# Linear attention with a sine-gated MLP on one core: the first quarter of w_in by a hardware queue in fp32, the first k by the software queue, and x stored batch by batch

## The chip, the cores and the metric

The kernel runs on 1 core of one Trainium2 chip, in one launch. The metric is the device time in microseconds (us) of one execution. The core has five engines that work side by side: PE (matrix products), DVE, ACT and POOL (elementwise work), and SP, which here only starts transfers. Loads and stores are moved by 16 DMA engines. SP and ACT start transfers on hardware queues; POOL starts them on the software queue, and a transfer on it may change the type from fp32 to bf16 on its way.

## The reference

```python
# q, k, v: [4 batches, 8 heads, 768 positions, 64]; lam: [8]
for b in range(12):                      # blocks of 64 positions
    intra = (qb @ kb.T * Dmask) @ vb     # Dmask[i, j] = lam ** (i - j) for i >= j, else 0
    inter = (qb * lam ** (i + 1)) @ kv_state
    out[block] = intra + inter
    kv_state = lam ** 64 * kv_state + (kb * lam ** (63 - i)).T @ vb
x = out as [3072 tokens, 512]
h = x @ w_in                             # w_in: [512, 2048]
s = sin(alpha * h)
g = h + s * s / (alpha + 1e-9)
y = g @ w_out                            # w_out: [2048, 512]; y is the result, fp32
```

All inputs and the result are fp32 in memory. The kernel computes its products in bf16.

## The kernel before, in words

The 768 positions are cut into 6 chunks of 128 (NT = 6). One chunk of all 4 batches is a group of 512 tokens. For each group the attention gives x (`xt`), then 16 units `hidden(g, f)` (f from 0 to 15) compute h for 128 columns of w_in each, and `project(g, m, part)` multiplies the result `gall` with w_out. The order of all work is written out by hand: the text of the kernel is the order of each engine's instructions. The attention of chunk t + 1 and the projections of group g - 1 are placed between the hidden units of group g.

**Start-up (lines 66 to 129).** SP's hardware queue loads k of chunk 0, batch 0 as fp32 into `raw_k`, ACT's hardware queue loads q of batch 0 into `raw_q` (L79 to L81). POOL then starts six loads of 128 KB (bf16 in SBUF), k and q of batches 1 to 3 (L112 to L114), two loads of v with 256 KB each (batches 0 and 1, then 2 and 3, L115), w_in's first quarter in two halves (L117, L118), and its other three quarters (L119). The software queue works through them in this order.

**Chunk 0 (lines 499 to 543).** DVE casts `raw_k` to bf16 (L502) and scales `raw_q` (L503). For each batch, PE transposes k and q (`turn`, L261), ACT copies the results to SBUF (L267), PE computes the scores and DVE multiplies them by the decay table C0 into an `STm` tile (`scores1`, L286; pool `work`, 3 buffers, L49). `outs` (L297) multiplies `STm` by v and writes x of that batch into `xt`: batch 0 by ACT (L304), batches 1 to 3 by DVE (L306). There are 4 batches and 3 `STm` buffers. `spin` (L493) issues matrix products on a constant tile whose results are not used; such calls stand at the beginning (nine of 512 columns) and between the steps. `decay_tables` (L170) computes, on ACT, tables of powers of lam; L128, four of its instructions, is read nowhere. L538 loads ACT's table for the sine.

**Hidden units (L429).** One unit is 4 products of 512 columns (L433, one for each 128 rows of w_in), the sine on ACT (L436), a square on ACT (L441) or on DVE (L449; `squarer`, L422, chooses), and the sum on DVE into `gall` (L450). `xt` is laid out as [128, 4 parts of the feature dimension, 512 tokens], so that a product reads 512 adjacent elements per partition. In group 0, units 1, 3, 5, 7, 9 and 13 have their square on DVE.

**POOL after the start-up (lines 544 to 554).** w_out's first quarter, a product `kdec` (L226) of chunk 0, loads of chunk 1, another `kdec`, the table C64 (L187), further quarters of w_out and loads of chunk 1, in this order; casts of the state (L330) follow. POOL waits where it stands for a tile that has not landed, and starts no transfer that is written behind.

Of the kernel before, what the change touches and what calls it, by code (L numbers as in the profile page):

```python
# [15 lines left out]
def kernel(  # L16
# [26 lines left out]
    consts = ctx.enter_context(tc.tile_pool(name="consts", bufs=1))  # L43
    wpool = ctx.enter_context(tc.tile_pool(name="wts", bufs=1))
    rawp = ctx.enter_context(tc.tile_pool(name="raw", bufs=1))
    qkp = ctx.enter_context(tc.tile_pool(name="qk", bufs=2))
    vp = ctx.enter_context(tc.tile_pool(name="vv", bufs=3))
    trp = ctx.enter_context(tc.tile_pool(name="trans", bufs=2))
    work = ctx.enter_context(tc.tile_pool(name="work", bufs=3))  # L49
    kdp = ctx.enter_context(tc.tile_pool(name="kdec", bufs=2))  # L50
    kvp = ctx.enter_context(tc.tile_pool(name="kvstate", bufs=2))
    xtp = ctx.enter_context(tc.tile_pool(name="xt", bufs=2))
# [14 lines left out]
    HALF = (LO, HI)  # L67
# [3 lines left out]
    qn, kn, vn = {}, {}, {}  # L71
    NAT = {"k": (kn, k), "q": (qn, q), "v": (vn, v)}
# [2 lines left out]
        for d, nm, p in ((qn, "qn", qkp), (kn, "kn", qkp), (vn, "vn", vp)):  # L75
            d[t] = p.tile([P, B, H, D], BF16, name=nm)

    raw = {}
    for nm, eng in (("k0", nc.sync), ("q0", nc.scalar)):  # L79
        raw[nm] = rawp.tile([P, H, D], FP32, name=f"raw_{nm}")  # L80
        eng.dma_start(out=raw[nm][:], in_=NAT[nm[0]][1][0, :, 0:T, :].rearrange("h p e -> p h e"))  # L81
    alpha_fp = consts.tile([NFC, P], FP32, name="alpha_fp")

    w_in_sb = [wpool.tile([P, NDC, 512], BF16, name=f"w_in{i}") for i in range(4)]
    w_out_sb = [wpool.tile([P, 4, DM], BF16, name=f"w_out{i}") for i in range(4)]

    def load_w_in(i, w0=0, w1=512):
        w = slice(512 * i + w0, 512 * i + w1)
        nc.gpsimd.dma_start(out=w_in_sb[i][:, :, w0:w1], in_=moe_w_in[:, w].rearrange("(c p) g -> p c g", p=P))

    def load_w_out(i):
        nc.gpsimd.dma_start(out=w_out_sb[i][:],
# [2 lines left out]
    def load(t, nm, b0, b1):  # L95
        dst, src = NAT[nm]
        to = dst[t][:, b0:b1, :, :].rearrange("p b h e -> p (b h) e")
        by_head = src[b0:b1, :, t * T:(t + 1) * T, :].rearrange("b h p e -> p (b h) e")
        n = H * (b1 - b0)
        if t and nm != "v" and b0 == 2:  # L100
            nc.gpsimd.dma_start(out=to[:, 0:n - 1, :], in_=by_head[:, 1:n, :])
            nc.gpsimd.dma_start(out=to[:, n - 1:n, :], in_=by_head[:, 0:1, :])
        else:
            nc.gpsimd.dma_start(out=to, in_=by_head)  # L104
# [4 lines left out]
    dist = consts.tile([P, T], FP32, name="dist")  # L109
    nc.gpsimd.iota(out=dist[:], pattern=[[1, T]], base=0, channel_multiplier=-1,  # L110
                   allow_small_or_imprecise_dtypes=True)
    for b in range(1, B):  # L112
        for nm in "kq":
            load(0, nm, b, b + 1)  # L114
    for b in (0, 2):  # L115
        load(0, "v", b, b + 2)
    load_w_in(0, 0, 256)  # L117
    load_w_in(0, 256, 512)  # L118
    for i in range(1, 4):  # L119
        load_w_in(i)  # L120

# [26 lines left out]
    lnlam = consts.tile([P, H + 2], FP32, name="lnlam")  # L148
# [15 lines left out]
    Etab = consts.tile([P, HP, T], FP32, name="Etab")  # L164
    Eb = Etab[:, :, 0:D].unsqueeze(1).broadcast_to([P, 2, HP, D])
    L64 = consts.tile([P, 2, HP], FP32, name="L64")
    L128 = consts.tile([P, 2, HP], FP32, name="L128")
    later = {}

    def decay_tables():  # L170
        nc.scalar.copy(out=lnlam[:, H:H + 2], in_=lnlam[:, 0:2])
        later["R128"] = powers("R128", 2, lnlam[:], [P, H + 2])
        later["NE64"] = powers("NE64", 3, lnlam[:].rearrange("p (hp hd) -> p hd hp", hd=2), [P, 2, HE])
        later["R64"] = powers("R64", 4, lnlam[:], [P, H + 2])
        for L, n in ((L128, T), (L64, D)):
            for pr in range(2):
                for hd, half in enumerate(HALF):
                    nc.scalar.activation(out=L[half, pr, :], in_=lnlam[half, pr + hd:pr + hd + H - 1:2],
                                         func=ACTF.Exp, scale=float(n))

    def etab(*cs):
        for c in cs:
# [11 lines left out]
    V, G, A = nc.vector, nc.gpsimd, nc.scalar  # L194
    xt = {}
# [17 lines left out]
        return SB[2 if blk else t % 2]  # L213

    def new_xt(t):
        xt[t] = xtp.tile([P, NDC, GRP], BF16, name="xt")

    def xview(t):
        return xt[t][:].rearrange("p c (b k i) -> p b k c i", b=B, k=2)

    def decay_k(t, b0, b1):
        if t not in kdec:
# [48 lines left out]
    def halves(hd):  # L271
        return slice(hd * D, (hd + 1) * D)
# [24 lines left out]
    def outs(t, b, n, eng=None):  # L297
        O = bank("O_ps", n)[:].rearrange("p (c i) -> p c i", c=HP)
        for h in range(H):
            nc.tensor.matmul(out=O[halves(h % 2), h // 2, :], lhsT=vn[t][:, b, h, :], rhs=STm[t, b][:, h % 2, h // 2, :],  # L300
                             start=(h < 2), stop=True, skip_group_check=True)
        x = xt[t][:, :, b * T:(b + 1) * T]
        if eng is nc.scalar:
            nc.scalar.copy(out=x, in_=O)  # L304
        else:
            nc.vector.tensor_tensor(out=x, in0=O, in1=Etab[:], op=ALU.mult)  # L306
# [114 lines left out]

    def squarer(g, f):  # L422
        if g == 0:
            return V if f in (1, 3, 5, 7, 9, 13) else A
        return A

    H0 = (0, 1, 2, 3, 5, 6, 7, 0, 1, 2, 5, 0, 1, 2, 0, 1)
# [1 line left out]
    def hidden(g, f, between=None):  # L429
        hps = bank("hps", H0[f] if g == 0 else (5, 6, 4)[f] if g == 1 and f < 3 else AB[0] if g == 1 and f == 15 else AB[f + 1] if g == 2 and f < 2 else (1, 0, 2)[(f + 2) % 3] if g == 1 and f > 6 else HB[(16 * g + f + 1) % 3])  # L430
        w = w_in_sb[f // 4]
        for c in range(NDC):
            nc.tensor.matmul(out=hps[:], lhsT=w[:, c, (f % 4) * P:(f % 4 + 1) * P],  # L433
                             rhs=xt[g][:, c, :], start=(c == 0), stop=(c == NDC - 1))
# [58 lines left out]
    def spin(n, bk, cols=256):  # L493
        ps = bank("hps", bk)
        for _ in range(n):
            nc.tensor.matmul(out=ps[:, 0:cols], lhsT=fill[:, 0:P], rhs=fill[:, 0:cols], start=True, stop=True)  # L496
# [1 line left out]

    new_xt(0)
    new_turned(0)  # L500
    spin(9, 0, 512)
    nc.vector.tensor_copy(out=kn[0][:, 0, :, :], in_=raw["k0"][:])  # L502
    nc.vector.tensor_tensor(out=qn[0][:, 0, :, :], in0=raw["q0"][:], op=ALU.mult,  # L503
                            in1=Rq[:].unsqueeze(2).broadcast_to([P, H, D]))
    nc.vector.tensor_tensor(out=C0[:], in0=tri[:].unsqueeze(1).unsqueeze(1).broadcast_to([P, 2, HP, T]),
                            in1=NE[:].unsqueeze(3).broadcast_to([P, 2, HP, T]), op=ALU.mult)
# [29 lines left out]
    outs(0, 1, 1)  # L536
    warm = consts.tile([P, 1], FP32, name="warm")
    nc.scalar.activation(out=warm[:], in_=lnlam[:, 0:1], func=ACTF.Sin)  # L538
    spin(2, 6)
    outs(0, 2, 2)  # L540
    spin(2, 6)
    outs(0, 3, 0)
    spin(5, 6)
    load_w_out(0)
    decay_k(0, 0, 2)
    for nm in "kq":
# [185 lines left out]
```

## Time and profile before

| | |
|---|---|
| median of 3 runs | 210.94 us (210.92 to 210.99) |
| the profiled execution's own time | 210.92 us |
| its span in the profile | 209.1 us |
| PE busy | 197.3 us (94%) |
| ACT busy | 144.4 us (69%) |
| DVE busy | 135.3 us (65%) |
| POOL busy | 93.6 us (45%) |
| software queue (q0) | 13.37 MB, 77200 packets |

The span runs from the first to the last instruction of the program; 1.8 us of the execution lie around it. The profile is one execution on the chip. A line of its timeline gives the start in us, the duration, the engine, the line of the kernel and the operation, the tile written and the tiles read, and in brackets how long the engine stood idle before and what ended that. "PEld" is PE's weight load, which runs beside its products. A group "x4" of adjacent instructions stands in one line. In the view by stretches, each line gives for each engine the us it was busy, then the granted clock of PE, the us that the DMA engines were busy with packets (packets of several queues or several in flight add up), and the GB/s that were written at the destination.

### The profile page before, as it was taken

How to read it: one execution, taken by the hardware profiler on the slowest of the kernel's cores; microseconds unless marked ns; L12 is line 12 of the kernel's file. 1: busy time of each engine (PE TensorE's matmuls, PEld its weight loads, DVE VectorE, ACT ScalarE, POOL GpSimd, SP SyncE). 2: the span in 40 equal slices, each digit the busy share in tenths (PEclk: the TensorE clock that was granted, in tenths of full speed). 3: DMA queues.
4: the chain of work that ended last, by engine and by line, in shares of the span. 5: the costliest groups of instructions: out<-in, count | busy, mean ns of one | idle time of the engine just before them, and what ended most of it. 6: DMA issues, size and time to landing. Idle time of an engine off the chain costs nothing.

```text
span 209.1 us, 5355 instructions
## 1 busy us (share of the span) xinstructions
PE 197.3 (94%) x2203; PEld 97.7 (47%) x2233; DVE 135.3 (65%) x260; ACT 144.4 (69%) x242; POOL 93.6 (45%) x99
## 2 busy tenths in 40 slices
PE   6679998999989999999999999999999999999993
PEld 2444445554444544445444444445444444444462
DVE  4674997665599878978548978557867544444000
ACT  4699999216988898765776775776675787887121
POOL 8999949897639941998942207002000000000000
PEclk9999999999999999999999999999999999999999
DMA  5999999999999999999999908601101101110212
GB/s 103 155 159 206 205 164 181 182 180 155 159 268 71 147 147 170 91 164 183 142 148 191 183 4 136 168 0 53 50 3 53 50 0 50 52 53 0 100 60 92
DMA packets 98920, 24.47 MB, mean 117 GB/s; under 512 B 91072, under 2 KB 95952, under 8 KB 98896
## 3 DMA queue, kind: packets, MB, share of 16 engines
q0 software_dynamic: 77200, 13.37, 85.2%
q1 hardware_dynamic: 20512, 10.50, 23.8%
q10 hardware_dynamic: 1184, 0.27, 0.6%
q8 instruction: 17, 0.28, 0.5%
q14 instruction: 7, 0.06, 0.1%
HBM read 27.28 MB, written 6.29 MB: 161 GB/s over the span
## 4 chain that ended last, share of the span: by engine, by line
PE 66%; DMA 15%; ACT 5%; POOL 5%; DVE 4%; issue 3%; POOLq 0%; ACTq 0%
PE ops L461 32%; PE hps L433 27%; DMA kn<-in_k_dram 7%; DMA w_out<-in_moe_w_out_dram 5%; DMA qn<-in_q_dram 3%; ACT s_sb L436 2%; DVE S L327 2%; POOL kdec L226 2%; PE hps L485 2%; ACT s L441 2%; PE O_ps L380 2%; DVE gall L450 1%; PE F_ps L366 1%; PE O_ps L408 1%; PE KV_ps L349 1%
## 5 line engine op out<-in xcount | busy, mean ns | idle before, releaser
L450 DVE SCALAR_TENSOR_TENSOR gall<-s,r_sb,hps 128x512 bf16<-128x512 bf16 x96 | 70.8, 744 | 42.1 <-ACT s L441 41.8
L433 PE MATMUL hps<-xt,w_in 128*128 128x512 bf16 x370 | 94.9, 379 | 1.6 <-ACT QKT L282 0.3
L461 PE MATMUL ops<-w_out,gall 128*128 128x512 bf16 x352 | 90.4, 379 | 2.0 <-DMA w_out<-in_moe_w_out_dram 0.7
L436 ACT ACTIVATE s_sb<-hps,alpha_sb 128x512 bf16<-128x512 f32 x96 | 65.4, 685 | 33.6 <-PE hps L433 33.0
L441 ACT ACTIVATE s<-s_sb 128x512 bf16<-128x512 bf16 x90 | 56.7, 630 | 2.9
L433 PEld LDWEIGHTS <-w_in 128*128 128x128 bf16 x384 | 36.6, 98 | 44.0 <-issue 1.5
L461 PEld LDWEIGHTS <-gall 128*128 128x128 bf16 x368 | 35.0, 98 | 41.4 <-issue 1.3
L330 POOL CAST sb<-S 128x512 bf16<-128x512 f32 x20 | 12.2, 617 | 37.5 <-DVE S L327 34.2
L226 POOL TENSOR_TENSOR kdec<-kn,R 128x1024 bf16<-128x1024 bf16 x12 | 22.8, 1908 | 5.2 <-DMA kn<-in_k_dram 4.9
L327 DVE SCALAR_TENSOR_TENSOR S<-S,L,KV_ps 128x128 f32<-128x128 f32 x72 | 20.0, 342 | 0.6 <-PE KV_ps L349 0.6
L415 DVE TENSOR_TENSOR xt<-O_ps,Etab 128x512 bf16<-128x512 f32 x20 | 12.8, 682 | 3.5 <-PE O_ps L408 3.5
L104 POOL DMA_DIRECT2D vn<-in_v_dram x12 | 14.3, 1191 | 0.0
L470 ACT COPY o_sb<-ops 128x512 f32<-128x512 f32 x11 | 6.4, 578 | 10.2 <-PE ops L461 10.2
L373 DVE TENSOR_TENSOR STm<-F_ps,C 128x512 bf16<-128x512 f32 x20 | 12.8, 681 | 0.8 <-PE F_ps L366 0.8
L468 DVE COPY o_sb<-ops 128x512 f32<-128x512 f32 x12 | 8.3, 689 | 4.1 <-PE ops L461 4.1
L267 ACT COPY QKT<-T_ps 128x512 bf16<-128x512 bf16 x10 | 5.7, 586 | 6.4 <-PE T_ps L265 6.4
L398 POOL COPY QKT<-QKT 64x2 bf16<-64x2 bf16 x3 | 0.6, 186 | 19.4 <-PE O_ps L380 11.2
L496 PE MATMUL hps<-fill 128*128 128x256 bf16 (+1 forms) x32 | 7.6, 358 | 1.5 <-DVE fill L123 1.5
L104 POOL DMA_DIRECT2D kn<-in_k_dram x8 | 8.8, 1100 | 0.3 <-issue 0.3
L104 POOL DMA_DIRECT2D qn<-in_q_dram x8 | 8.6, 1077 | 0.0
L380 PEld LDWEIGHTS <-sb 64*64 64x64 bf16 x320 | 4.2, 108 | 4.3 <-issue 4.2
L294 DVE TENSOR_TENSOR STm<-F_ps,C 128x512 bf16<-128x512 f32 x8 | 5.0, 682 | 1.7 <-PE O_ps L300 1.1
(69 smaller groups left out, 109.4 us busy)
## 6 DMA issues: line engine op xcount, KB each, us to landing
out_dram<-o_sb SPq DMA_DIRECT2D x23, 256.0 KB, 2.5
vn<-in_v_dram POOLq DMA_DIRECT2D x12, 256.0 KB, 7.7
w_out<-in_moe_w_out_dram POOLq DMA_DIRECT2D x4, 512.0 KB, 12.5
w_in<-in_moe_w_in_dram POOLq DMA_DIRECT2D x3, 512.0 KB, 12.0
kn<-in_k_dram POOLq DMA_DIRECT2D x5, 256.0 KB, 8.1
qn<-in_q_dram POOLq DMA_DIRECT2D x5, 256.0 KB, 7.8
kn<-in_k_dram POOLq DMA_DIRECT2D x5, 240.0 KB, 8.6
qn<-in_q_dram POOLq DMA_DIRECT2D x5, 240.0 KB, 9.6
```

The source lines that it names most:

```text
L104: nc.gpsimd.dma_start(out=to, in_=by_head)
L226: nc.gpsimd.tensor_tensor(out=kdec[t][:, b0:b1, :, :], in0=kn[t][:, b0:b1, :, :], in1=R[:, o:o + H].unsqueeze(1).unsqueeze(3).broadcast_to ...
L327: nc.vector.scalar_tensor_tensor(out=S[:, bs, hp, :], in0=old[:, bs, hp, :], scalar=decay[:, pr, hp:hp + 1], in1=ps[:, :, hp, :], op0=ALU. ...
L330: nc.gpsimd.tensor_copy(out=dst[:, bs], in_=S[:, bs])
L373: nc.vector.tensor_tensor(out=st[:, hd], in0=att["F", t, pr, hd], op=ALU.mult, in1=of_mask(C64, t, pr, hd).unsqueeze(1).broadcast_to([P, 2 ...
L380: nc.tensor.matmul(out=att["O", t, pr, blk][halves(h % 2), u, h // 2, :], lhsT=home(t, blk)[halves(half), 2 * pr + m // HP, m % HP, :], rh ...
L415: nc.vector.tensor_tensor(out=xview(t)[:, 2 * pr:2 * pr + 2, blk, :, :], in0=att["O", t, pr, blk], in1=Eb, op=ALU.mult)
L433: nc.tensor.matmul(out=hps[:], lhsT=w[:, c, (f % 4) * P:(f % 4 + 1) * P], rhs=xt[g][:, c, :], start=(c == 0), stop=(c == NDC - 1))
L436: nc.scalar.activation(out=s_sb[:], in_=hps[:], func=ACTF.Sin, scale=alpha_sb[:, f:f + 1])
L441: nc.scalar.activation(out=s2[:], in_=s_sb[:], func=ACTF.Square)
L450: nc.vector.scalar_tensor_tensor(out=gall[g][:, f, :], in0=s2[:], scalar=r_sb[:, f:f + 1], in1=hps[:], op0=ALU.mult, op1=ALU.add)
L461: nc.tensor.matmul(out=ops[:], lhsT=gall[g][:, f, m * P:(m + 1) * P], rhs=w_out_sb[part][:, f % 4, :], start=(f == 0), stop=(f == NFC - 1))
```

## The change

- w_in's first quarter (columns 0 to 511) comes by two transfers of SP's hardware queue as fp32 into `raw_w` (1 MB), at the place of `raw_k`'s transfer. POOL casts it to bf16 in four instructions, which stand where the two software loads stood.
- k of batch 0 comes by the software queue, in bf16, ahead of the six others. DVE's cast of `raw_k` goes.
- `xt` is laid out as [128, 4 batches, 4 parts, 128 tokens]. A product of a hidden unit reads 4 stretches of 128 elements. The first unit is computed in two parts: 4 products for batches 0 to 2 (384 columns), then 4 for batch 3 (128 columns).
- The pool `work` has 4 buffers.
- `squarer`: units 6 and 8 in place of 7 have their square on DVE (7 units in place of 6).
- `decay_tables` leaves out L128.
- `spin`: 12 in place of 9 products of 512 columns at the beginning; before `outs(0, 2)` 4 in place of 2, none in place of 2 before `outs(0, 3)`, 1 in place of 5 behind it.

```diff
-    work = ctx.enter_context(tc.tile_pool(name="work", bufs=3))
+    work = ctx.enter_context(tc.tile_pool(name="work", bufs=4))
...
-    raw = {}
-    for nm, eng in (("k0", nc.sync), ("q0", nc.scalar)):
-        raw[nm] = rawp.tile([P, H, D], FP32, name=f"raw_{nm}")
-        eng.dma_start(out=raw[nm][:], in_=NAT[nm[0]][1][0, :, 0:T, :].rearrange("h p e -> p h e"))
+    raw_q = rawp.tile([P, H, D], FP32, name="raw_q")
+    nc.scalar.dma_start(out=raw_q[:], in_=q[0, :, 0:T, :].rearrange("h p e -> p h e"))
+    raw_w = rawp.tile([P, NDC, 512], FP32, name="raw_w")
+    for c in range(0, NDC, 2):
+        nc.sync.dma_start(out=raw_w[:, c:c + 2, :],
+                          in_=moe_w_in[c * P:(c + 2) * P, 0:512].rearrange("(c p) g -> p c g", p=P))
...
+    load(0, "k", 0, 1)
     for b in range(1, B):
         for nm in "kq":
             load(0, nm, b, b + 1)
     for b in (0, 2):
         load(0, "v", b, b + 2)
-    load_w_in(0, 0, 256)
-    load_w_in(0, 256, 512)
+    for c in range(NDC):
+        nc.gpsimd.tensor_copy(out=w_in_sb[0][:, c, :], in_=raw_w[:, c, :])
...
-        for L, n in ((L128, T), (L64, D)):
-            for pr in range(2):
-                for hd, half in enumerate(HALF):
-                    nc.scalar.activation(out=L[half, pr, :], in_=lnlam[half, pr + hd:pr + hd + H - 1:2],
-                                         func=ACTF.Exp, scale=float(n))
+        for pr in range(2):
+            for hd, half in enumerate(HALF):
+                nc.scalar.activation(out=L64[half, pr, :], in_=lnlam[half, pr + hd:pr + hd + H - 1:2],
+                                     func=ACTF.Exp, scale=float(D))
...
-        xt[t] = xtp.tile([P, NDC, GRP], BF16, name="xt")
+        xt[t] = xtp.tile([P, B, NDC, T], BF16, name="xt")
...
-        x = xt[t][:, :, b * T:(b + 1) * T]
+        x = xt[t][:, b]
...
-            return V if f in (1, 3, 5, 7, 9, 13) else A
+            return V if f in (1, 3, 5, 6, 8, 9, 13) else A
...
-        for c in range(NDC):
-            nc.tensor.matmul(out=hps[:], lhsT=w[:, c, (f % 4) * P:(f % 4 + 1) * P],
-                             rhs=xt[g][:, c, :], start=(c == 0), stop=(c == NDC - 1))
+        by_batch = hps[:].rearrange("p (b i) -> p b i", b=B)
+        for bs in (slice(0, B - 1), slice(B - 1, B)) if g + f == 0 else (slice(0, B),):
+            for c in range(NDC):
+                nc.tensor.matmul(out=by_batch[:, bs], lhsT=w[:, c, (f % 4) * P:(f % 4 + 1) * P],
+                                 rhs=xt[g][:, bs, c, :], start=(c == 0), stop=(c == NDC - 1))
...
-    spin(9, 0, 512)
-    nc.vector.tensor_copy(out=kn[0][:, 0, :, :], in_=raw["k0"][:])
-    nc.vector.tensor_tensor(out=qn[0][:, 0, :, :], in0=raw["q0"][:], op=ALU.mult,
+    spin(12, 0, 512)
+    nc.vector.tensor_tensor(out=qn[0][:, 0, :, :], in0=raw_q[:], op=ALU.mult,
...
-    spin(2, 6)
+    spin(4, 6)
     outs(0, 2, 2)
-    spin(2, 6)
     outs(0, 3, 0)
-    spin(5, 6)
+    spin(1, 6)
```

More of the change, by code (lines that the diff above doesn't have):

```diff
@@ L85, with load_w_in @@
     w_out_sb = [wpool.tile([P, 4, DM], BF16, name=f"w_out{i}") for i in range(4)]
-    def load_w_in(i, w0=0, w1=512):
-        w = slice(512 * i + w0, 512 * i + w1)
-        nc.gpsimd.dma_start(out=w_in_sb[i][:, :, w0:w1], in_=moe_w_in[:, w].rearrange("(c p) g -> p c g", p=P))
+    def load_w_in(i):
+        nc.gpsimd.dma_start(out=w_in_sb[i][:],
+                            in_=moe_w_in[:, 512 * i:512 * (i + 1)].rearrange("(c p) g -> p c g", p=P))
     def load_w_out(i):
@@ L166 @@
     L64 = consts.tile([P, 2, HP], FP32, name="L64")
-    L128 = consts.tile([P, 2, HP], FP32, name="L128")
     later = {}
@@ L215, in new_xt @@
     def new_xt(t):
-        xt[t] = xtp.tile([P, NDC, GRP], BF16, name="xt")
+        xt[t] = xtp.tile([P, B, NDC, T], BF16, name="xt")
     def xview(t):
-        return xt[t][:].rearrange("p c (b k i) -> p b k c i", b=B, k=2)
+        return xt[t][:].rearrange("p b c (k i) -> p b k c i", k=2)
     def decay_k(t, b0, b1):
```

## The prediction

> **What bounds the kernel now.** I read the page first: its span, and the chain of work that ended last.
>
> ```profile
> span 209.1 us, 5355 instructions
> ...
> PE 66%; DMA 15%; ACT 5%; POOL 5%; DVE 4%; issue 3%; POOLq 0%; ACTq 0%
> ```
>
> The chain is mostly PE. The same chain in order of time shows where the 15% of DMA lie: all of it ends by 46.5 us.
>
> ```profile
> 4.14 5.83 DMA qn<-in_q_dram
> ...
> 15.79 14.53 DMA kn<-in_k_dram
> ...
> 36.03 10.44 DMA w_out<-in_moe_w_out_dram
> 46.51 0.38 PE ops L461
> ```
>
> So a change to the loads counts only as far as it moves PE by 46.5 us; behind that no load is on the chain, and I carry the shift to the end. All edits but the layout of x act ahead of that. Next the timeline, from the last loads of the start-up to the first hidden units.
>
> ```profile
> 8.21 0.23 PEld L265 LDWEIGHTS <-qn 128*128 128x128 bf16 x4 [0.42 <-DMA qn<-in_q_dram]
> 9.11 0.23 PEld L265 LDWEIGHTS <-kn 128*128 128x128 bf16 x4 [0.34 <-DMA kn<-in_k_dram]
> 10.01 0.23 PEld L265 LDWEIGHTS <-qn 128*128 128x128 bf16 x4 [0.35 <-DMA qn<-in_q_dram]
> ...
> 13.63 0.48 PEld L300 LDWEIGHTS <-vn 128*64 128x64 bf16 x16 [0.28 <-DMA vn<-in_v_dram]
> 14.08 1.29 DVE L294 TENSOR_TENSOR STm<-F_ps,C 128x512 bf16<-128x512 f32 x2 [1.07 <-PE O_ps L300]
> 15.29 1.87 DVE L306 TENSOR_TENSOR xt<-O_ps,Etab 128x512 bf16<-128x512 f32 x3
> 15.31 0.25 PEld L300 LDWEIGHTS <-vn 128*64 128x64 bf16 x8 [1.00 <-DMA vn<-in_v_dram]
> 15.31 0.41 PE L300 MATMUL O_ps<-STm,vn 128*64 128x128 bf16 x8 [0.72 <-DMA vn<-in_v_dram]
> 15.88 0.59 ACT L304 CAST xt<-O_ps 128x512 bf16<-128x512 f32 x1
> 16.48 1.28 ACT L538 ACT_TABLE_LOAD   x1
> 17.31 6.29 PE L433 MATMUL hps<-xt,w_in 128*128 128x512 bf16 x27 [0.27 <-DVE xt L306]
> ```
>
> PE waits for one load after another, 0.90 us apart for 128 KB, and for the last v until 15.31. From there DVE makes three x tiles, the last ends at 17.16, and PE starts the hidden units 0.15 later. From 17.31 PE hardly stops. The later waits for loads:
>
> ```profile
> 20.83 2.27 PEld L433 LDWEIGHTS <-w_in 128*128 128x128 bf16 x12 [0.40 <-DMA w_in<-in_moe_w_in_dram]
> ...
> 36.42 1.89 PE L461 MATMUL ops<-w_out,gall 128*128 128x512 bf16 x8 [0.50 <-DMA w_out<-in_moe_w_out_dram]
> 38.15 0.61 PE L279 MATMUL T_ps<-iden,kn 128*128 128x128 bf16 x8
> 40.68 1.04 PE L461 MATMUL ops<-w_out,gall 128*128 128x512 bf16 x4
> 42.34 1.89 PE L461 MATMUL ops<-w_out,gall 128*128 128x512 bf16 x7 [0.25 <-DMA w_out<-in_moe_w_out_dram]
> ```
>
> Two products of eight 512-column steps show the pace: (1.89 - 1.04) / 4 = 0.21 us a step.
>
> **The change part by part.** Three terms make the sum: when the last v lands, how soon after it the second hidden unit starts, and which later waits go.
>
> *Term 1, the last v.* All software loads stand in one queue, so what is put ahead of v delays it. The view by stretches gives the rates.
>
> ```profile
> 2.00:4.00 2.00, 2.00 (x7) 0.62 (x6) 0.48 (x4) 0.99 (x2) 2.00 (x3) 1.00 0.48 104
> 4.00:6.00 2.00, 1.45 (x10) 0.58 (x8) 1.26 (x3) 1.95 (x5) 2.00 (x4) 1.00 1.76 229
> 6.00:8.00 2.00, 0.95 (x12) 0.56 (x10) 1.52 (x2) 0.92 (x2) 2.00 (x3) 1.00 2.42 154
> 16.00:26.00 10.00, 9.63 (x66) 4.55 (x68) 7.30 (x13) 9.36 (x16) 9.89 (x9) 1.00 1.26 206
> 61.00:62.00 1.00, 0.78 (x4) 0.26 (x3) 1.00 (x5) 1.00 (x4) 0.20 (x1) 1.00 1.07 408
> ```
>
> The new load `raw_w` is 1.05 MB in rows of 2 KB. No row shows such a load. The stores alone at 61 to 62 move 408 GB/s, which makes 2.6 us; the weights at 16 to 26 write 206 GB/s in bf16 and so read 412 in fp32, which makes 2.6 too. I take 2.6. k of batch 0 on the software queue adds 0.90 (the spacing above). `raw_k`, 0.26 MB, leaves the hardware queue: at the 229 GB/s of 4 to 6 us that is 1.1. And the DMA engines were busy for only 0.48 us of 2 to 4, so a part of `raw_w` fits into time that stood empty: between 0 and 1.5 us, and I take 0.75, since transfers start only after 2 us. Together 2.6 + 0.90 - 1.1 - 0.75 = **1.65 us later**; the ends are 2.4 (nothing absorbed) and 0.9 (all of it). q, k and v all move by this, so the steps between them keep their order, and v stays last: the last `STm` is done before it.
>
> The Trainium skill, page "DMA: Bandwidth & Descriptors", section "Issuing engines are not separate DMA queues", says that transfers of all issuing engines end on the same 16 DMA engines and interleave there. By it the hardware queue relieves nothing; no row here separates the queues.
>
> *Term 2, from the last v to the second unit.* Before: from 15.31 to 17.31 + 4 x 0.21 = 18.17, or 2.86. After: the fourth `work` buffer takes away the wait of 1.07 at 14.08, which was for the first `STm` to be read, so DVE makes x of batch 1 ahead of v's landing. The product for batch 2 ends at 0.41, DVE needs 1.87 / 3 = 0.62 (to 1.08 with 0.05 between), PE starts 0.15 later (1.23) with 384 columns x 4 at 0.16 = 0.65 (to 1.88). Batch 3's x ends at 1.70, hidden by that. Its four steps of 128 columns: eight such take 0.61 in the row of 38.15 and 4 take 0.40 (below), so 0.21 for four more; done at 2.1 to 2.15. Gain **0.72 us**; 0.55 if the small steps cost 0.4.
>
> *Term 3, the later waits.* Behind v the software queue no longer carries w_in's first quarter (0.52 MB at 206 GB/s, 2.5 us): everything behind lands 2.5 - 1.65 = 0.85 us earlier, while PE arrives 1.65 - 0.72 = 0.93 later. All three waits go. What is late next: at 20.83 the weight load waited but PE's products ran on almost unbroken (27 are recorded, 28 stand in the code: 28 x 0.215 = 6.0 of 6.29, and the last one's tail is 0.2), so 0.08. Of the 0.50, the transposes of 38.15 use bank 0, which DVE's sum of unit 14 frees:
>
> ```profile
> 37.01 1.40 DVE L450 SCALAR_TENSOR_TENSOR gall<-s,r_sb,hps 128x512 bf16<-128x512 bf16 x2
> ```
>
> The first of the two ends at 37.71; with 0.13 to PE the transposes can come at 37.84, not 37.65. So 0.31 is gained. The 0.25 goes whole. Sum **0.65**; the ends are 0.3 (only the bank-free part) and 0.93 (no new wait, and 0.1 at 46.5).
>
> *Edits costed at nothing, and their cover.* POOL issues one load more and casts instead of issuing two halves.
>
> ```profile
> 1.33 1.08 POOL L104 DMA_DIRECT2D kn<-in_k_dram  x1 [0.27 <-issue]
> 7.23 0.40 PE L265 MATMUL T_ps<-iden,qn 128*128 128x128 bf16 x4 [1.05 <-DVE qn L503]
> 9.10 3.77 POOL L89 DMA_DIRECT2D w_in<-in_moe_w_in_dram  x5
> 14.16 1.70 ACT L178 ACTIVATE L<-lnlam 64x4 f32<-64x4 f32 x8
> 32.34 1.16 POOL L330 CAST sb<-S 128x512 bf16<-128x512 f32 x2
> ```
>
> Four casts of this shape take 2.3 us, two issues 1.5, and the load of k 0.9: POOL reaches the second quarter of w_in at about 12.3, 1.7 us later than now, while the queue is busy with v until it lands at 17. First casts at 10: `raw_w` has landed. If a cast took 1.2 us, POOL would be at 14.7 and still ahead. `kdec` and the next loads come 1.7 us later as well, behind a queue that holds 14.5 us of work (the chain's row at 15.79). SP's third transfer, alpha, is needed only beside k of batch 3. L128 takes 0.85 off ACT, which then reaches x of batch 0 and the sine table earlier; v covers it. DVE's dropped cast, the spins (PE waits for loads there) and the moved square (0.63 off ACT, 0.42 onto DVE; neither holds PE between 17 and 36) are hidden by PE's own work. For the strided x read no row exists. Four separate products of 128 columns cost 4 x 0.053 = 0.21 by the transposes above, as much as one of 512, so I take nothing for reading in four stretches; a gain is excluded, as the number of columns is the same.
>
> Sum against the profiled execution's 210.92 (span 209.1 and 1.8 around it; the median of the runs is 210.94): 210.92 + 1.65 - 0.72 - 0.65 = **211.2 us**.
>
> **Rivals.**
> - *The load hides in the empty time.* For: 2 to 4 us holds 1.5 idle us, and `raw_k` leaves. Then v is 0.9 late: 0.9 - 0.72 - 0.65 = -0.5, 210.4; with 0.93 won behind it, 210.2. Against: the empty time begins before any transfer can start.
> - *All queues share and nothing is absorbed* (the skill's rule above, paid in full). Place: the last v. Price: 2.4 - 0.72 - 0.65 = +1.0, 212.0; with 0.3 won behind, 212.3. It decides as soon as v is more than 1.8 us late. For: at 4 to 6 us the packets already fill 1.76 of 2.00. Against: the idle share just ahead.
> - *PE's clock falls back.* The first nine spins:
>
> ```profile
> 1.45 3.56 PE L496 MATMUL hps<-fill 128*128 128x512 bf16 x9 [1.45 <-DVE fill L123]
> ```
>
>   They took 0.395 us each against 0.215 later. Twelve end near 5.7, k of batch 0 lands near 8, and PE is idle between. If the first 3 us of the hidden units ran at that pace: 7.6 steps x 0.18 = +1.4, 212.6. Against: the granted clock reads 1.00 at 6 to 8 us now, where PE is busy for 0.95 of 2.00. The Trainium skill, page "TensorE: Matmul & The Clock Gate", section "The HAM clock gate", has the clock halved after about 3.4 us of idleness; the gap here is 2.3.
> - *Strided x is read more slowly.* 384 products; 5 ns each, which the rounding of the rows would hide, are +1.9, 213.1. For: no row of such a read exists. Against: the transposes' pace.
>
> **How the numbers follow.** The forecast, 211.2 (own range 210.7 to 211.8), has 0.42; the hidden load 0.25; full sharing 0.25; clock 0.04; strided reads 0.04. The range 210.2 to 212.2 reaches over the ends of term 1 and leaves out the last two and the far end of sharing. A measurement of this kernel can tell about 0.2% (0.42 us) from no change. Faster by more: the hidden load and a little of the forecast, 0.25. Slower by more: sharing, clock, strided reads and the forecast's upper edge, 0.37. Within: 0.38.
>
> **What would show it.** Term 1: the wait of PE's weight loads for the last v ends at about 17.0, not 15.3, and k of batch 0 is awaited until near 8. Term 2: DVE's wait for O_ps ahead of `STm` is gone, and the second unit starts 2.1 to 2.2 us after v. Term 3: no wait for w_in or w_out at 36 and 42. If v lands by 16.2 the first rival holds; if after 17.2 the second. Products of 512 columns over 0.216 us apart would show strided reads, a granted clock under 1.00 the clock. A wait for POOL's casts would make the cover wrong.

## The result, and the profile after

The kernel after takes **216.82 us** (median of 4 runs, 216.48 to 217.49) against 210.93 (210.92 to 210.99) before: a ratio of 1.0283, 95% interval 1.0257 to 1.0308. The forecast was 211.2 with a range to 212.2. Lines of the code lie a little lower after the change: `outs` writes x at L305 and L307, the hidden units are L436 to L453, the projections L464.

The profiled execution after is the slowest of the four, 0.67 us over the median; what follows accounts for its span. Its page (217.49 us): span, the row of PE's granted clock, and the chain that ended last.

```profile
span 215.7 us, 5448 instructions
...
PEclk9959999999999999999999999999999999999999
...
PE 68%; DVE 10%; ACT 6%; issue 3%; DVEq 0%; ACTq 0%
```

DVE has 10% of the chain where it had 4%, and one slice has half the clock. That no DMA stands on the chain says nothing of the first loads: in order of time, its first row is the following one, and nothing ahead of it could be followed back.

```profile
22.55 0.14 issue
```

The timeline after, from the first loads to the first hidden unit:

```profile
1.45 5.21 PE L499 MATMUL hps<-fill 128*128 128x512 bf16 x12 [1.45 <-DVE fill L126]
...
6.38 0.21 ACT L152 ACTIVATE lnlam<-lam_bc 128x8 f32<-128x8 f32 x1 [3.42 <-DMA lam_bc<-in_lam_dram]
10.74 0.69 DVE L505 TENSOR_TENSOR qn<-raw_q,Rq 128x512 bf16<-128x512 f32 x1 [3.77 <-DMA raw_q<-in_q_dram]
11.37 0.61 PE L266 MATMUL T_ps<-iden,kn 128*128 128x128 bf16 x4 [4.71 <-DMA kn<-in_k_dram]
11.61 1.15 POOL L106 DMA_DIRECT2D vn<-in_v_dram  x1 [2.80 <-DMA kn<-in_k_dram]
...
17.97 0.39 PE L266 MATMUL T_ps<-iden,qn 128*128 128x128 bf16 x4
...
20.66 1.89 DVE L307 TENSOR_TENSOR xt<-O_ps,Etab 128x512 bf16<-128x512 f32 x3
...
20.80 0.64 PE L301 MATMUL O_ps<-STm,vn 128*64 128x128 bf16 x16
...
22.69 6.21 PE L436 MATMUL hps<-xt,w_in 128*128 128x384 bf16 x32 [1.04 <-DVE xt L307]
```

Everything that a load feeds is late from the beginning. PE's spins end at 1.45 + 5.21 = 6.66; then it stands for 4.71 us and gets the first k at 11.37 (5.56 before). The four transposes there take 0.61, those at 17.97 take 0.39. The tile view of v after gives the time from issue to landing of the second load:

```profile
DMA to landing us min/median/max: 8.1/8.1/8.1
```

Issued at 11.61, it landed at 19.7, where the last v was there at 15.31 before: 4.4 us later. POOL issued it 3.6 us later than before, as it stood 2.80 for a k, but the software queue did not run dry meanwhile: the stretches from 9.5 to 14 us below have 155 to 157 GB/s. PE did not wait for this v: it came to the product with the second v at 20.80, after transposes and scores at half the clock. (With the clock at 1.00, in e7 below, it waits for this v until 19.4.) The first hidden unit starts 5.38 us later (22.69 against 17.31), and 1.0 of that lies behind v's landing. The view by stretches after (columns as described with the profile before):

```profile
2.00:4.00 2.00, 2.00 (x7) 0.60 (x6) 0.48 (x4) 0.95 (x1) 2.00 (x3) 1.00 0.23 42
4.00:6.00 2.00, 2.00 (x6) 0.72 (x5) 0.00 (x0) 0.00 (x0) 2.00 (x4) 1.00 0.74 199
...
9.50:10.00 0.50, 0.00 (x0) 0.00 (x0) 0.00 (x0) 0.00 (x0) 0.00 (x0) 0.86 2.28 157
...
10.50:14.00 3.50, 2.63 (x20) 2.23 (x20) 1.83 (x2) 1.66 (x3) 2.39 (x4) 0.50 2.43 155
```

From 2 to 4 us, in the empty time on which the forecast counted, less moves than before: 42 GB/s where it was 104, and the DMA engines are busy for 0.23 us of 2. The granted clock falls inside 9.5 to 10, near 9.9, and is 0.50 until 16.7. The DMA view of 5 to 8 us after has by queue:

```profile
q1 hardware_dynamic: 385, 0.71, 68.2%
q10 hardware_dynamic: 857, 0.21, 32.2%
q0 software_dynamic: 134, 0.02, 8.8%
```

q1 is `raw_w` and q10 is `raw_q`. The software queue (q0), which before the change had been at work since 4 and moved 3370 packets in these 3 us, gets 134 through, none of them before 7.2 us. Later in the same trace, first the chain in order of time, then the timeline of the same place:

```profile
34.01 2.00 DVE s L452
...
36.91 1.04 PE hps L436 x4
```

```profile
25.81 0.71 DVE L452 TENSOR_TENSOR s<-s_sb 128x512 bf16<-128x512 bf16 x1
...
27.95 0.98 DVE L452 TENSOR_TENSOR s<-s_sb 128x512 bf16<-128x512 bf16 x1
...
33.82 1.90 POOL L227 TENSOR_TENSOR kdec<-kn,R 128x1024 bf16<-128x1024 bf16 x1
33.92 2.08 DVE L452 TENSOR_TENSOR s<-s_sb 128x512 bf16<-128x512 bf16 x1
34.06 1.02 PE L436 MATMUL hps<-xt,w_in 128*128 128x512 bf16 x4 [0.75 <-DVE gall L453]
...
36.91 0.38 PE L436 MATMUL hps<-xt,w_in 128*128 128x512 bf16 x1 [0.96 <-DVE gall L453]
...
43.19 1.90 PE L464 MATMUL ops<-w_out,gall 128*128 128x512 bf16 x8
44.34 1.40 DVE L453 SCALAR_TENSOR_TENSOR gall<-s,r_sb,hps 128x512 bf16<-128x512 bf16 x2
45.23 0.61 PE L280 MATMUL T_ps<-iden,kn 128*128 128x128 bf16 x8
```

A square on DVE that elsewhere takes 0.42 lasts 2.08, beside POOL's `kdec`, and is on the chain with 2.00. PE waits for DVE, and its delay against before grows from 5.38 to 7.3 us (the unit at 36.91 stood at 29.57). Not all of this is that one square: PE waits 0.75 for DVE at 34.06 already, behind squares of 0.71 and 0.98, which ran beside POOL's `kdec` of 24.30 and its table product of 27.37; the 0.96 at 36.91 is the wait behind the long square. The product at 43.19 has no wait for w_out in front of it (36.42 before, so 6.77 late), and the transposes behind are 7.08 late (45.23 against 38.15): that is 0.31 back, from the bank that DVE frees at 45.04.

So the 6.6 us of the span are 4.4 for the last v, 1.0 between v and the first hidden unit, 1.95 within the hidden units, and about -0.7 for the later waits.

### The profile page after: what moved, and what is told of

It is laid out like the page before. It is cut to its first block, busy times and chain, and to the rows that moved or that the text cites. A ratio compares the mean times of both kernels' runs of the same rounds, so it can differ in the third digit from the quotient of the medians.

```text
span 215.7 us, 5448 instructions
## 1 busy us (share of the span) xinstructions
PE 202.2 (94%) x2236; PEld 99.5 (46%) x2236; DVE 137.2 (64%) x260; ACT 143.2 (66%) x237; POOL 95.5 (44%) x102
## 4 chain that ended last, share of the span: by engine, by line
PE 68%; DVE 10%; ACT 6%; issue 3%; DVEq 0%; ACTq 0%
PE ops L464 33%; PE hps L436 28%; DVE gall L453 4%; ACT s_sb L439 3%; DVE s L452 2%; DVE S L328 2%; ACT s L444 2%; PE O_ps L381 2%; PE hps L488 2%; PE F_ps L367 1%; PE KV_ps L350 1%; PE O_ps L409 1%; DVE xt L416 1%; ACT QKT L283 1%; DVE STm L374 1%
## 5 line engine op out<-in xcount | busy, mean ns | idle before, releaser
L436 PE MATMUL hps<-xt,w_in 128*128 128x512 bf16 (+2 forms) x388 | 96.0, 377 | 3.3 <-DVE gall L453 2.0
L453 DVE SCALAR_TENSOR_TENSOR gall<-s,r_sb,hps 128x512 bf16<-128x512 bf16 x96 | 70.7, 744 | 41.7 <-ACT s L444 41.1
L464 PE MATMUL ops<-w_out,gall 128*128 128x512 bf16 x368 | 92.2, 379 | 0.2 <-DVE o_sb L471 0.2
L436 PEld LDWEIGHTS <-w_in 128*128 128x128 bf16 x388 | 36.8, 98 | 46.5 <-issue 3.0
L444 ACT ACTIVATE s<-s_sb 128x512 bf16<-128x512 bf16 x89 | 56.0, 630 | 2.8
L464 PEld LDWEIGHTS <-gall 128*128 128x128 bf16 x368 | 34.7, 98 | 40.7 <-issue 0.6
L499 PE MATMUL hps<-fill 128*128 128x256 bf16 (+1 forms) x31 | 9.4, 441 | 1.5 <-DVE fill L126 1.5
L106 POOL DMA_DIRECT2D kn<-in_k_dram x9 | 9.7, 1076 | 0.3 <-issue 0.3
L399 POOL COPY QKT<-QKT 64x2 bf16<-64x2 bf16 x3 | 0.6, 185 | 19.4 <-PE O_ps L381 11.2
L266 PE MATMUL T_ps<-iden,kn 128*128 128x128 bf16 x16 | 2.2, 288 | 4.7 <-DMA kn<-in_k_dram 4.7
```

What stands on the lines that cost most here:

```text
L436: nc.tensor.matmul(out=by_batch[:, bs], lhsT=w[:, c, (f % 4) * P:(f % 4 + 1) * P], rhs=xt[g][:, bs, c, :], start=(c == 0), stop=(c == NDC ...
L453: nc.vector.scalar_tensor_tensor(out=gall[g][:, f, :], in0=s2[:], scalar=r_sb[:, f:f + 1], in1=hps[:], op0=ALU.mult, op1=ALU.add)
L464: nc.tensor.matmul(out=ops[:], lhsT=gall[g][:, f, m * P:(m + 1) * P], rhs=w_out_sb[part][:, f % 4, :], start=(f == 0), stop=(f == NFC - 1))
```

## The experiments

**Theory** after the two traces: the hardware transfer `raw_w` holds up the other loads (4.4); the clock's fall costs most of the 1.0; the squares meet POOL's products because everything is late (2.0); the split of the first unit gains nothing because its bank (0) is the one that x of batch 3 is read from until DVE is through. **Rivals**: POOL's extra work or the first k's new place makes the loads late; the moved square is wrong by itself; `raw_w` is slow only because its rows are strided, or only because it comes so early.

Times of each kernel's profile (us), and the medians. Each ratio is to before on the same chip, whose medians were 210.87 (e1 to e4), 210.84 (e5 to e8) and 210.79 (e9 to e12).

| kernel | first k transposed | first hidden unit | span | median us | ratio to before, 95% interval |
|---|---|---|---|---|---|
| before | 5.56 | 17.31 | 209.1 | 210.93 | |
| after | 11.37 | 22.69 | 215.7 | 216.82 | 1.0283 (1.0257 to 1.0308) |
| e1_w_by_software | 6.55 | 17.16 | 210.3 | 211.24 | 1.0033 (1.0009 to 1.0057) |
| e2_square_back | 11.32 | 23.93 | 215.6 | 216.00 | 1.0255 (1.0220 to 1.0291) |
| e3_bank7 | 11.27 | 21.30 | 215.0 | 216.86 | 1.0291 (1.0274 to 1.0309) |
| e4_contiguous_rows | 11.08 | 21.38 | 214.5 | 216.28 | one run |
| e5_raw_w_held | 6.38 | 22.94 | 215.6 | 216.99 | 1.0290 (1.0261 to 1.0318) |
| e6_software_split_bank7 | 5.63 | 16.90 | 209.5 | 211.41 | 1.0034 (1.0011 to 1.0056) |
| e7_more_spins | 11.24 | 21.47 | 214.5 | 216.47 | 1.0263 (1.0236 to 1.0291) |
| e8_software_spins | 6.14 | 17.31 | 209.2 | 211.23 | 1.0032 (1.0006 to 1.0059) |
| e9_terms_together | 11.27 | 21.23 | 213.7 | 215.49 | 1.0224 (1.0208 to 1.0239) |
| e10_small_packets | 6.55 | 22.37 | 215.0 | 216.90 | 1.0297 (1.0283 to 1.0311) |
| e11_kdec_in_four | 11.73 | 21.58 | 214.3 | 216.06 | 1.0253 (1.0239 to 1.0267) |
| e12_split_alone | 5.55 | 17.19 | 209.2 | 210.86 | 1.0014 (0.9993 to 1.0034) |

**e1_w_by_software**: after, with w_in's first quarter by the software queue as before.

```diff
-    raw_w = rawp.tile([P, NDC, 512], FP32, name="raw_w")
-    for c in range(0, NDC, 2):
-        nc.sync.dma_start(out=raw_w[:, c:c + 2, :], ...
...
-    for c in range(NDC):
-        nc.gpsimd.tensor_copy(out=w_in_sb[0][:, c, :], in_=raw_w[:, c, :])
+    load_w_in(0, 0, 256)
+    load_w_in(0, 256, 512)
```

> The changed kernel, but w_in's first quarter comes by the software queue again, in two halves where the casts stood; no raw_w. Theory A (the 1 MB of the hardware queue holds up all loads behind it at the start): the first k lands about 7 us instead of 11.3, the last v about 16 instead of 20.4, the first hidden unit starts at 17 to 18.5 instead of 22.7, and the whole takes 211 to 213.5 us. Rival (k as the first software load is late by itself): k still lands after 10 us, the hidden units start after 21, and the whole stays above 215.

Nearly all of the loss is gone, as Theory A had it: 211.24. Rows of its timeline and one of its stretches:

```profile
15.27 0.64 PE L297 MATMUL O_ps<-STm,vn 128*64 128x128 bf16 x16 [0.54 <-DMA vn<-in_v_dram]
...
30.20 1.90 POOL L223 TENSOR_TENSOR kdec<-kn,R 128x1024 bf16<-128x1024 bf16 x1 [2.25 <-ACT s_sb L435]
31.30 1.07 DVE L448 TENSOR_TENSOR s<-s_sb 128x512 bf16<-128x512 bf16 x1
```

```profile
17.00:21.00 4.00, 3.84 (x14) 1.85 (x15) 0.70 (x2) 1.68 (x3) 4.00 (x4) 0.57 1.25 205
```

The last v is there at 15.27, as before the change (15.31), although k of batch 0 stands ahead of it in the queue: that part of the change costs nothing. The hidden units start at 17.16 but with a clock of 0.57, and by 25 us this profile is 1.45 us behind before. The last two rows are a square that meets a `kdec` there and takes 1.07.

**e2_square_back, e3_bank7, e4_contiguous_rows**: one edit each to the kernel after.

```diff
-            return V if f in (1, 3, 5, 6, 8, 9, 13) else A
+            return V if f in (1, 3, 5, 7, 9, 13) else A
```

> The changed kernel with the squares of group 0 as before (units 1, 3, 5, 7, 9, 13 on DVE). In the changed kernel DVE's square of unit 8 took 2.08 us, from 33.92, beside POOL's kdec product from 33.82 to 35.72, and PE's lag behind the kernel before grew from 5.3 to 7.3 us there. Theory B (a bf16 square on DVE stands still while POOL runs a product): the long square goes, the lag stays near 5.3, and the whole takes 214.5 to 215.2 us, 2 less than the changed kernel. Rival (the square of unit 7 meets the same product, or PE's lag has another source): 216.3 to 217.3.

In e2's timeline the `kdec` that held a square for 2.08 meets only a short piece of one:

```profile
34.73 1.90 POOL L227 TENSOR_TENSOR kdec<-kn,R 128x1024 bf16<-128x1024 bf16 x1
...
36.16 0.75 DVE L452 TENSOR_TENSOR s<-s_sb 128x512 bf16<-128x512 bf16 x1
```

The delay grows by 0.57 there (from 6.62 at the first unit to 7.19 at 36.76), not 1.95, but the median, which lies between the two expected ranges, gains only 0.8 of the 2, and the intervals of the two ratios overlap. In this profile, the slowest of four, the clock was at half for 10.2 us (10.5 to 20.8) where it was 6.8 after, so the units started 1.2 after those of the kernel after. The mechanism held in the trace, the size on the median did not.

```diff
-    outs(0, 3, 0)
+    outs(0, 3, 7)
```

> The changed kernel with the product of v for batch 3 in PSUM bank 7 instead of bank 0, which the first hidden unit writes. Theory C (the first unit's part for batches 0 to 2 waits for bank 0, which DVE reads for x of batch 3, so the split gains nothing): the first unit then starts about 0.65 us before the last x of batch 3 is done, 22.05 instead of 22.69, the second unit starts 0.5 to 0.65 earlier, and the whole is 0.3 to 0.7 us shorter. Rival (the first unit waits for x itself or for the casts of w_in): no change of the start, 216.3 to 217.3.

In e3 PE started the hidden units 1.29 us after the last x products (20.01 to 21.30), where the kernel after needs 1.89 (20.80 to 22.69): the bank was the reason, 0.60 of the 0.72 of term 2. The total did not move: the earlier units met POOL worse, with a square of 1.31 where the kernel after has 0.71, and the one of 2.08 stayed. Rows of e3:

```profile
23.52 1.92 POOL L227 TENSOR_TENSOR kdec<-kn,R 128x1024 bf16<-128x1024 bf16 x1
24.42 1.31 DVE L452 TENSOR_TENSOR s<-s_sb 128x512 bf16<-128x512 bf16 x1
```

e4 lets `raw_w` read adjacent rows, which lie in w_out; h of its first quarter is thus from other numbers.

```diff
-                          in_=moe_w_in[c * P:(c + 2) * P, 0:512].rearrange("(c p) g -> p c g", p=P))
+                          in_=moe_w_out[c * P:(c + 2) * P, 0:512].rearrange("(c p) g -> p c g", p=P))
```

> The changed kernel, but raw_w is read from the first 512 rows of w_out instead of the first quarter of w_in's columns, so that h of the first quarter is computed from other numbers: the same 512 rows of 2 KB, but adjacent in memory instead of one every 8 KB. Theory D (the hardware queue is slow at the start because its rows lie far apart in memory): raw_w is through by 5.5 us, q lands before 8 instead of at 10.7, the first k before 9 instead of at 11.3, and the hidden units start 2 to 3 us earlier. Rival (the queue is slow at that time whatever it reads): within 0.5 us of the changed kernel everywhere.

Stretches of e4:

```profile
2.00:4.00 2.00, 2.00 (x7) 0.63 (x6) 0.48 (x4) 0.96 (x1) 2.00 (x3) 1.00 0.32 50
4.00:6.00 2.00, 2.00 (x6) 0.75 (x5) 0.00 (x0) 0.00 (x0) 2.00 (x4) 1.00 0.93 271
```

A little faster from 4 us on, no faster before (50 GB/s), and the first k lands 0.3 sooner. Strided rows are not the cause of the late loads. The units start 1.3 sooner than after (21.38), but in this execution the clock was at half for only 3.4 us (10.4 to 13.9).

**e5_raw_w_held**: `raw_w` is asked for only when DVE has scaled q, near 6 us.

```diff
+    nc.vector.memset(raw_w[:, :, 0:1], 0.0)
...
     nc.sync.dma_start(out=alpha_fp[:], in_=moe_alpha.rearrange("(f p) -> f p", p=P))
+    for c in range(0, NDC, 2):
+        nc.sync.dma_start(out=raw_w[:, c:c + 2, :], ...
```

> The kernel after, but the raw first quarter of w_in is asked for only when DVE has scaled the queries, behind alpha on SyncE's queue; the casts and the other three quarters of w_in follow it on GpSimd as before. Theory (early transfers are slow, whatever they read, and those queued behind them are late): raw_q and lam land some 2 to 4 us earlier than after's, the first part of k near 5.5 us instead of 11.3, raw_w moves fast once it starts near 8 us, the first hidden unit starts at 18.5 to 19.5 us and the whole takes 212 to 214. Rival (the transfer itself is slow or holds the other queues up at whatever time): the hidden units start after 21 us and the whole takes 215 or more.

The rival holds: 216.99. The early part is as wished (first k at 6.38), and then the same loss comes later. The DMA view of e5, q0 alone from 5 to 8 us, then both queues from 9 to 13, and PE's wait:

```profile
q0 software_dynamic: 3295, 0.42, 217.4%
```

```profile
q1 hardware_dynamic: 442, 0.86, 72.4%
q0 software_dynamic: 900, 0.11, 44.2%
```

```profile
14.58 0.61 PE L259 MATMUL T_ps<-iden,qn 128*128 128x128 bf16 x4 [5.23 <-DMA qn<-in_q_dram]
```

The software queue alone moves 0.42 MB in 3 us, 138 GB/s. Beside `raw_w` it moves 0.11 MB in 4 us, 28 GB/s, a fifth. `raw_w` itself gets 215 GB/s, half of what the forecast took. At these rates, an estimate from the rows, its 1.05 MB last 4.9 us, and the software queue loses four fifths of that time: 3.9 us. PE waits 5.23 for one q, and the clock falls in that wait too (near 13.0).

**e10_small_packets**: e5 with `raw_w` in packets of 512 B.

```diff
-    for c in range(0, NDC, 2):
-        nc.sync.dma_start(out=raw_w[:, c:c + 2, :],
-                          in_=moe_w_in[c * P:(c + 2) * P, 0:512].rearrange("(c p) g -> p c g", p=P))
+    for g in range(0, 512, 128):
+        nc.sync.dma_start(out=raw_w[:, :, g:g + 128],
+                          in_=moe_w_in[:, g:g + 128].rearrange("(c p) g -> p c g", p=P))
```

> e5_raw_w_held with the raw first quarter asked for in four column blocks, so that a row gives packets of 512 B instead of 2 KB. In e5 the software queue moved 900 packets between 9 and 13 us beside 442 of raw_w, two for one, 28 GB/s where it had 138 GB/s alone. Theory (the DMA engines take turns by packets): four times as many turns, the software queue keeps 80 GB/s or more beside raw_w, the q of batch 1 or 2 that landed at 14.5 lands by 12.5, the first hidden unit starts before 21.8 and the whole takes 214.3 to 215.8. Rival (the queues share by bytes or time): the software queue stays at 25 to 40 GB/s, first hidden unit after 22.3, 216.5 or more.

The same stretch, 9 to 13 us, in e10:

```profile
q1 hardware_dynamic: 1339, 0.67, 71.6%
q0 software_dynamic: 1456, 0.18, 71.1%
```

The rate is neither side's: the software queue keeps 46 GB/s, more than in e5 and less than 80, nearly packet for packet now. The first unit (22.37) and the time are the rival's: `raw_w` slows to 168 GB/s and so lasts 6.2 us; 6.2 x (1 - 46/138) = 4.2 us, nearly the same price, and the time is the same 216.9. By the Trainium skill, page "DMA: Bandwidth & Descriptors", section "Queues, rings and completion order", an engine goes round the queues and takes a whole packet from each, one of several descriptors. An estimate from that has to assume that the packets that the profile counts are what takes turns. Equal turns then give `raw_w` 16 times the bytes of the software queue in e5 (2048 to 128) and 4 times in e10; the traces have 7.8, which differs, and 3.7, which agrees.

**e7_more_spins**: after, with spins that keep PE at work until the first k is there.

```diff
-    spin(12, 0, 512)
+    spin(34, 0, 512)
...
-    spin(4, 6)
+    spin(2, 6)
     outs(0, 2, 2)
+    spin(2, 6)
     outs(0, 3, 0)
-    spin(1, 6)
+    spin(5, 6)
```

> The kernel after with 34 spinning matmuls at the start instead of 12 and 2, 2 and 5 later instead of 4, 0 and 1, so that TensorE has work until the first k has landed. If the granted clock's fall before the first transposes costs time: granted clock 1.00, transposes of 128 columns at 0.40 instead of 0.61, and 0.5 to 0.9 less than after, about 216.0. Rival (the late landings alone set the time, and the clock's fall lies beside them): within 0.2 of after's 216.8.

One stretch of e7:

```profile
8.00:12.00 4.00, 4.00 (x26) 1.92 (x23) 1.37 (x2) 0.63 (x3) 1.33 (x2) 1.00 2.27 169
```

The clock stays at 1.00, and the first hidden unit starts 2.1 after v's landing at 19.4 (2.00 before, 3.0 after). The profile wins 1.2 us by that point, of which 0.3 is v landing sooner; the median wins 0.35, less than expected and more than the rival's 0.2, and the intervals of the two ratios overlap.

**e11_kdec_in_four**: e7 with each `kdec` as four instructions of a batch and half of its heads.

```diff
-        nc.gpsimd.tensor_tensor(out=kdec[t][:, b0:b1, :, :], ...
+        for b in range(b0, b1):
+            for h in (0, H // 2):
+                nc.gpsimd.tensor_tensor(out=kdec[t][:, b, h:h + H // 2, :], ...
```

> e7_more_spins with each of GpSimd's kdec products issued as four of a quarter each (a batch and half of its heads). Theory (a square on DVE that meets a GpSimd product waits for that whole instruction): no square over 1.1 us where one took 2.08, PE's 1.7 of waits for DVE's gall fall to 0.6 or less, 216.5 becomes 215.3 to 216.0. Rival (the square is slowed for as long as GpSimd works there at all): a square of about 2 us stays and the time stays within 0.2 of 216.5.

```profile
23.57 2.34 POOL L229 TENSOR_TENSOR kdec<-kn,R 128x256 bf16<-128x256 bf16 x4
24.70 1.50 DVE L454 TENSOR_TENSOR s<-s_sb 128x512 bf16<-128x512 bf16 x1
...
33.52 2.50 POOL L229 TENSOR_TENSOR kdec<-kn,R 128x256 bf16<-128x256 bf16 x4
33.62 0.78 DVE L454 TENSOR_TENSOR s<-s_sb 128x512 bf16<-128x512 bf16 x1
```

The square at 33.62, which took 2.08 in e7, now lasts 0.78, while POOL's group runs to 36.02: it waited for one instruction, not for POOL to be through. The one at 24.70 (1.50, over the 1.1 expected) stood until the last two of POOL's four were through. POOL's four take 2.3 to 2.5 us where one took 1.9, PE still waits 1.5 us for DVE, and the median, 0.4 under e7's with overlapping intervals, just misses the expected one. The Trainium skill, page "SBUF — State Buffer", section "SBUF: two separate sides", says that DVE and GpSimd share a pair of ports as a lock that one instruction holds to its end. The traces agree: in every run, each square that a `kdec` lengthens ends 0.27 to 0.30 us after an instruction of POOL's ends (33.82 + 1.90 = 35.72 against 33.92 + 2.08 = 36.00 after).

**e8_software_spins and e6_software_split_bank7**: e1 with the spins of before; e6 also has the squares of before and `outs(0, 3, 7)`.

```diff
-    spin(12, 0, 512)
+    spin(9, 0, 512)
...
-    spin(4, 6)
+    spin(2, 6)
     outs(0, 2, 2)
+    spin(2, 6)
     outs(0, 3, 0)
-    spin(1, 6)
+    spin(5, 6)
```

> e1_w_by_software with the spins of before (9, 2, 2, 5), the squares still divided as after. If the 1.45 us that e1 lost within the first hidden units was its clock's fall: granted clock 1.00 and 210.0 to 210.8. Rival (the loss has another cause, such as the square beside kdec): 211.0 to 211.4 as e1.

> The kernel after with the first quarter of w_in by the software queue in two parts as before, the squares divided as before, the last group of x k products in bank 7 instead of bank 0, and the spins of before (9, 2, 2, 5): what is left of the change is x batch by batch, the first hidden unit in two parts and the four work buffers. Theory: the 0.6 that bank 7 gave between the last v and the second hidden unit is kept, no square runs beside GpSimd's kdec, and the whole takes 210.0 to 210.6. Rival (the later w_in and w_out, which the software queue again brings late, take back what is gained): 210.7 to 211.2.

e8's profile has the clock at 1.00 and the span of before (209.2 against 209.1), so in that execution e1's loss was the clock. The medians of e1 and e8 are equal and the rival's range held, because e1's profile is not its usual execution: of ten, seven have a mean clock of 1.00 and take 210.76 to 211.51, and the three with 0.992, the profiled one among them, take 212.04 to 212.97. e6 missed both of its intervals: its units start 0.41 sooner than before, and then PE waits 0.6 for DVE's sum behind a square of 0.96, beside POOL's table product. With the load on the software queue and the clock at 1.00 the moved square costs nothing: no `kdec` lengthens a square of e8, and PE never waits for DVE's sums there up to 50 us. (e1's profile, at the lower clock, has the one of 1.07 and a wait of 0.2.)

**e9_terms_together**: e7 with the squares of before and bank 7 (both edits as in e2 and e3).

> e7_more_spins (its spins keep the clock) with the squares divided as before and the last group of x k products in bank 7. Theory (the loss is the sum of late landings, squares held beside GpSimd's kdec, the clock, and the bank, and each can be taken away by itself): against e7's 216.5 the squares give back 1.4 to 2.0 and the bank 0.4 to 0.6, so 213.9 to 214.7, and what stays over 210.9 is the late landings alone, some 4.1 less the 0.7 of the later waits that are gone. Rival (another square or the banks collide in their place, as with bank 7 alone): 215.6 or more.

```profile
23.11 1.92 POOL L227 TENSOR_TENSOR kdec<-kn,R 128x1024 bf16<-128x1024 bf16 x1
24.36 0.97 DVE L452 TENSOR_TENSOR s<-s_sb 128x512 bf16<-128x512 bf16 x1
```

215.49: 1.0 less than e7, where 1.8 to 2.6 were expected, and nearly at the rival's 215.6. Of the 4.6 us over before in its span, 3.92 are there at the first hidden unit; 1.2 come within the hidden units, where PE waits 1.03 for DVE's sum at 32.94, behind squares that meet POOL at other places, such as this one; and the later waits give 0.6 back. The terms do not simply add: to move PE against POOL by 0.6 us gives other meetings.

**e12_split_alone**: before, and of the change only x batch by batch, the first unit in two parts, the four buffers, with bank 7.

> The kernel before with its own loads, squares and spins, and of the change only x batch by batch, the first hidden unit in two parts and four work buffers, with the last group of x k products in bank 7 instead of bank 0. Theory (the loads that come after limit it): the second hidden unit starts 0.4 to 0.7 sooner, and the two waits for w_out, 0.7 together before, grow by as much, so 210.6 to 210.9, no gain. Rival (the gain stays): 210.1 to 210.4.

```profile
14.83 1.70 ACT L178 ACTIVATE L<-lnlam 64x4 f32<-64x4 f32 x8
...
16.55 0.58 ACT L304 CAST xt<-O_ps 128x512 bf16<-128x512 f32 x1
17.19 2.11 PE L435 MATMUL hps<-xt,w_in 128*128 128x384 bf16 x13 [0.20 <-ACT xt L304]
```

The total is as the theory had it, the way is not. The units start only 0.12 sooner, because ACT, still busy with the table L128, copies x of batch 0 last. PE then loses 0.6 to a square, and the two waits for w_out, 0.7 together before, are gone instead of longer. No version was faster than before.

## Why the prediction was wrong, step by step

- **Term 1, the last v: the step that failed, in size.** 1.65 was forecast, 2.4 its upper end, 4.4 came. The part "+0.90 - 1.1" for the two k was right (e1: v at 15.27). "2.6 for `raw_w`" and "0.75 absorbed" were not. The 2.6 was a rate of stores alone and of the software queue alone. Beside each other, the hardware transfer gets 215 GB/s and leaves the software queue 28, which makes 3.9 us (e5), and asked for at the start it fills no empty time (42 GB/s from 2 to 4 us) while the software queue sends nothing before 7.2 us. e7 and e8, both at full clock, differ by 4.16 us at the first hidden unit; besides the spins only the way of w_in's first quarter is different.
- "No row here separates the queues" was not so. The DMA view of the kernel before separates them: from 4 to 5 us `raw_q` and `raw_k` move 0.27 MB and the software queue 96 packets of 128 B; from 5 to 6 it moves 920, and from 6 to 8, with those loads through, 1225 a us. In e1, with one hardware load less, it moves 172 packets already from 3 to 4 and 1037 from 4 to 5. The sign that a hardware load holds the software queue up was there before the change.
- The forecast compared where the bytes go. What counted is their place in the order: on the software queue w_in's first quarter stood behind v and cost v nothing; on a queue of its own it stands behind nothing.
- **Full sharing (212.0, 0.25)** was the rival in the right direction. Its point of decision, v over 1.8 late, was passed; its price assumed that two queues together move what one moves alone, some 410 GB/s; in e5 they write 244 (9 to 13 us).
- **The clock (0.04)** did fall back: I had put k of batch 0 near 8 us and so 2.3 us of idleness. k came at 11.37; the spins ended at 6.66, not near 5.7, and the clock fell near 9.9 (the stretch of 9.5 to 10 with 0.86), after 3.2 us. In other profiles it fell 2.4 us (e3) to 3.8 us (e2) after PE's last product. The Trainium skill's 3.4, cited there, lies between these. A gap of 2.3 was thus hardly safe. The fall cost 0.9 us in the profiles between v and the first unit (e7), 0.35 in the medians.
- **Term 2 (0.72): nothing came.** The wait of 1.07 ahead of `STm` went, as forecast, but the first unit's bank is that of `outs(0, 3, 0)`, so its first part had to wait for DVE's last x all the same. This is in the text of the kernel, and I did not compare the bank numbers. e3 shows 0.60 with another bank.
- **Term 3 (0.65): right**, about 0.7 in the trace (the delay falls from 7.34 to 6.61 by the product that stood at 47.87), with the transposes in bank 0 taking 0.31 of it back as worked out.
- **"The moved square: hidden" was wrong** in this kernel: with the squares of before, the delay grows by 0.57 within the hidden units in place of 1.95 (e2). The working asked only for busy time, not for what POOL does beside it. With the loads on time it was hidden (e8).
- **Strided x** cost nothing: four products that read x in four stretches take 1.04 us after, as four that read adjacent elements did before (40.68). That rival and the hidden load fell.

```profile
32.28 1.04 PE L436 MATMUL hps<-xt,w_in 128*128 128x512 bf16 x4
```

What stays open: why a hardware transfer asked for at the very start moves so little from 2 to 4 us and why the software queue then starts no packets; and how the medians' differences among the slower versions (after, e2, e3, e7, e9, e11) divide between clock and meetings, which differ from execution to execution; several of their intervals overlap.

## What to carry to other kernels

A second queue moved more bytes here (215 and 28 GB/s in e5, against 138 alone) and still took four fifths of the first queue's rate. So ask what the load stood behind, and what it now runs ahead of; in these runs a load of 1.05 MB on the second queue cost the small packets beside it most of its own length (3.9 of 4.9 us, 4.2 of 6.2). When a stage moves as a whole, look again at which instructions of DVE and POOL now meet, and which banks a "split" step shares with the step it should overlap.

## What the runs showed of the hardware

- Packets of 128 B on the software queue fall from 138 to 28 GB/s beside 2 KB packets of a hardware queue, and to 46 beside 512 B packets; the price of 1.05 MB, 3.9 and 4.2 us of the software queue by these rates, hardly differs between the two sizes.
- A bf16 square on DVE with both inputs in SBUF, 0.42 us alone, took up to 2.08 beside a product on POOL of 1.90.
- After PE stood idle, the granted clock was 0.50 for 3.4 us (e1, e4), 6.8 (after, e3, e5, e10) or 10.2 (e2): steps of about 3.4. In e1 it fell although PE had stood idle for 1.04 us only.
- Small stalls ahead of a later load are free: e12 was 0.83 us behind before at 35 us and 0.1 at the end, since before waits 0.7 for w_out there.
